# Scores of each batch's last 64 queries: four 64x64 products in place of two block-diagonal ones, in an attention + two-FFN kernel

## The chip, the cores and the metric

The kernel runs on one core of one Trainium2 chip. The metric is device time in microseconds (us) of one execution, the median of several runs; lower is better. The engines are named as in the profile: PE is TensorE's matmul, PEld its weight load, DVE is VectorE, ACT is ScalarE, POOL is GpSimd, SP issues DMAs.

## The reference

Four batches, eight heads, 576 positions, head size 64; then two feed-forward layers on the 2304 x 512 result.

```
scores = scale * q @ k.T                       # (4, 8, 576, 576), scale = 1/8
cum    = cumsum(max(s, 0))
scores = where(causal, -1e9, scores + min(-(cum_q - cum_k), 0))
attn   = softmax(scores) @ v
x = reshape(attn, (2304, 512))
x = ((x @ w_a) * (x @ w_b)) @ w_out            # d_ff 1536
h = x @ w_in                                   # d_ff 2048
out = (max(h, 0) + alpha * min(h, 0)) @ w_out2
```

## The kernel before

Positions are cut into four token blocks (512, 512, 512, 768 tokens). The feed-forward work of one block (`ffn`, and `ffn_seven` for the last block) is the stream that keeps PE busy; attention for the next block is fed into it in small steps. `attention(blk)` lists the steps for block blk: with a = blk, the first 512 queries of batch a (row blocks 0 to 3 of 128 queries: `s01`, `s23`), and with b = blk - 1, the last 64 queries of batch b (`s4`). Once the probabilities are ready, `two_av` or `av_b` multiplies them by v. The last batch's `s4` steps ride in the third block's stream, so the fourth block has no attention in it.

The change is about `s4(b, hp)`: the last QB = 64 queries of a batch, for a pair hp of heads, against all S = 576 keys. There are 4 batches x 4 pairs = 16 such steps. The pair's two heads lie on partitions 0 to 63 and 64 to 127 of the tile `kq` (columns 0 to 575 the keys, columns 576 to 703 the queries). The host lays the queries out block-diagonally (`last` in `kernel()`): columns 576 to 639 hold head 0's queries on partitions 0 to 63 and zero below, columns 640 to 703 hold head 1's on partitions 64 to 127 and zero above. So one 128x128 stationary operand gives both heads' scores, head j on output rows 64j to 64j+63. The keys go through in two halves of 288 columns, each into a PSUM bank of its own (L741). Operands are plain float32.

`soften` takes the scores out of PSUM. Its inner function `first()` issues one `tensor_tensor_reduce` per bank (L697): z = z - 0.125 * scores, with the row minimum into a column of `mn`; the issue is through the helper `dve`, so it shows up as L292 in the trace, as a CUSTOM_DVE_ANT_0 on z and a DVE_READ_ACCUMULATOR2_ANT on mn. With two columns in `mn`, one more 128x1 minimum joins them (L705). `rest()` does the exponential on ACT, the sum's reciprocal and the scaling; `turned` transposes on DVE (`zt`) and sends the result through DRAM (`zd`).

The order in which instructions are issued is made by a planner, `Order`, at build time. Each piece of work is a chain with a cost per engine (for a DVE operation of n elements, `run.dve + rate * n` ns with run.dve 90 or 155), and `run.pe(ns)` moves the planner's PE clock forward and lets it issue whatever fits (`pump`). From the second block on, a step is issued only when its inputs and its banks look ready by that clock (`possible`); feed-forward work goes ahead otherwise. `slot()` hands out PSUM banks from a ring: eight of them in the first attention, two (banks 0 and 1) afterwards; a bank is free again when its `reader` chain has ended.

Other PE lines that the prediction uses: L1248 to L1250 are the three products (high and low parts) of one feed-forward tile, 512 columns each, on the whole array. L557 and L563 (`q_k`) are the first batches' scores with 64 rows per head, so the two heads take one half of the array's rows each, into one bank each. L862 and L801 are probabilities times v with 128 rows and 64 output columns, the two heads on one half of the array's columns each.

Of the kernel before, what the change touches and what calls it, by code (L numbers as in the profile page):

```python
# [16 lines left out]
ALU = mybir.AluOpType  # L17
# [4 lines left out]
P = 128  # L22
# [4 lines left out]
BIG = 3.0e38  # L27
# [184 lines left out]
def attention_two_moe_kernel(  # L212
# [10 lines left out]
    nc = tc.nc  # L223
    B, S, _ = v.shape
# [8 lines left out]
    QB = S - QA  # L233
# [31 lines left out]
    run = Order()  # L265
# [8 lines left out]
    def act(o, i, func=AF.Copy, **k):  # L274
        yield {"act": run.act + 0.833 * size(o) + 93 * len(set(k) - {"scale"})}, SEEN
        nc.scalar.activation(o, i, func, **k)  # L276
# [13 lines left out]
    def dve(n, rate, f, *args, port=False, **k):  # L290
        yield {"dve2" if port else "dve": run.dve + rate * n}, SEEN
        f(*args, **k)  # L292
# [15 lines left out]
    def scale(o, i, s0, s1):  # L308
        n = size(o)
        eng = yield either(115 + 1.09 * n, dve2=run.dve + 0.52 * n), SEEN  # L310
        (nc.gpsimd if eng == "pool" else nc.vector).tensor_scalar(  # L311
            o, i, s0, s1, op0=ALU.mult, op1=ALU.mult
        )
# [123 lines left out]
    def slot():  # L437

        ring.append(ring.pop(0))
        if ring[-1] in reader:  # L440
            run.need(reader[ring[-1]])
        return ring[-1]
# [194 lines left out]
    def turned(b, h, rs, z):  # L637

        yield of_zt
        n = z.shape[1] // P  # L640
        zt = work.tile([P, 4 * n * 32], F32, name="zt", tag="zt", bufs=ZT)
        zd = dram.tile([4, P, n * 32], F32, name="zd", tag=f"zd{n}", bufs=8)
        yield from dve(
            n * P, 1.04, nc.vector.transpose, zt.rearrange("p (j t n) -> p j t n", j=4, n=32),
            z.rearrange("p (t j n) -> p j t n", j=4, n=32),
        )
        run.give(of_z[rs[0]], run.t)
        yield from dma(
            zd.rearrange("i (k j) m -> (i k) (j m)", j=4), zt
        )  # L650
        run.give(of_zt, run.t)
        if rs[0] == 4:
            yield of_pb
            pb_t[h] = raw.tile([P, 5 * P], F32, name="pb", tag="pb")
            o = pb_t[h].rearrange("p (i m) -> p i m", i=4)
        else:
            s0 = rs[0] * (rs[0] + 1) // 2 * 32
            o = pts[h % 4].rearrange("p (i m) -> p i m", i=4)[:, :, s0:s0 + n * 32]
        yield from dma(o, zd.rearrange("i p m -> p i m"))

    def soften(b, h, rs, srcs, *banks_read):

        got, masked = z_t[b, h, rs[0]]
        run.need(masked)
        z = got[0]
        k = len(rs)
        mn = small.tile([P, 2], F32, name="mn", tag="mn")
        sm = small.tile([P, 2], F32, name="sm", tag="sm")
        parts = []
        c = 0  # L670
        for i in rs:
            n = min(S, P * (i + 1))
            parts.append(z[:, c:c + n])
            c += n

        def rest():
            for i, p in enumerate(parts):
                yield from act(
                    p, p, AF.Exp, bias=mn[:, i:i + 1], scale=-1.0, accum_out=sm[:, i:i + 1]
                )  # L680
            for i in range(k):
                yield from dve(
                    1, 1, nc.vector.tensor_scalar, sm[:, i:i + 1], sm[:, i:i + 1], 1e-9, None,
                    op0=ALU.add,
                )
            yield from dve(1, 1, nc.vector.reciprocal, sm[:, 0:k], sm[:, 0:k])
            for i, p in enumerate(parts):
                yield from scale(p, p, sm[:, i:i + 1], 1.0)
            if b + (rs[0] == 4) >= TURN:
                e_t[b, h, rs[0]] = run.spawn(turned(b, h, rs, z), run.t)  # L690

        def first():
            c = 0
            for i, src in enumerate(srcs):
                n = src.shape[-1]
                p = z[:, c:c + n]
                yield from dve(  # L697
                    n, 1.04, nc.vector.tensor_tensor_reduce, p, src,
                    mask[:, QA - n:] if b < SUMS_PE and rs[0] < 4 else p, -0.125, BIG, ALU.add,
                    ALU.min, mn[:, i:i + 1],  # L700
                )
                c += n
            if len(parts) < len(srcs):
                yield from dve(
                    1, 1, nc.vector.tensor_tensor, mn[:, 0:1], mn[:, 0:1], mn[:, 1:2],  # L705
                    op=ALU.min, port=True,
                )
            if (b, h, rs[0]) == (SUMS_PE - 1, H - 1, 3):
                for i in range(KL):
                    run.give(of_kl, run.t)  # L710
            z_t[b, h, rs[0]] = z, run.spawn(rest(), run.t)

        got = run.spawn(first())
        z_t[b, h, rs[0]] = z, got
        for i in banks_read:
            reader[i] = got
# [16 lines left out]
    def s4(b, hp):  # L733


        got, ready = kq_t.pop((b, hp, 1))
        run.need(ready)
        at = [slot(), slot()]
        dst = [banks[i][:, 0:S // 2] for i in at]
        for j, d in enumerate(dst):  # L740
            nc.tensor.matmul(  # L741
                d, got[0][:, S:S + P], got[0][:, j * S // 2:(j + 1) * S // 2], start=True, stop=True
            )
            run.pe(4 * S // 2 / 2.4)
        run.give(of_kq)
        soften(b, hp, (4,), dst, *at)

# [184 lines left out]
    def attention(blk):  # L932
# [25 lines left out]
        for i in range(HP + 1):  # L958
# [9 lines left out]

            if has_a and a >= TURN:
                add(s4, i, b, i)  # L970
                add(s01, i, a, i)
                add(loads, i + 1, i + 1)
# [12 lines left out]
            elif has_a:  # L985
                add(s01, i, a, i)
                add(both, i, a, i, (2,))
                turns(0)
                add(both, i, a, i, (3,))
                add(s23, i, a, i, 2)  # L990
                last(j, 0)
                turns(1)
                last(j, 1)
                add(s23, i, a, i, 3)
                add(biases, i, b, i, (4,))
                add(loads, i + 1, i + 1)
                turns(2)
                add(both, i + 1, a, i + 1, (0, 1))
                add(two_av, j, a, b, j, blk)
                add(s4, i, b, i)  # L1000
            else:
                add(loads, i + 1, i + 1)
                add(s4, i, b, i)
                add(biases, i + 1, b, i + 1, (4,))
                last(i, 0)
                last(i, 1)
                if i == HP:
                    steps.extend([(lambda: None, ())] * TAIL)
                add(av_b, i - (blk >= TURN), b, i - (blk >= TURN), blk)
# [899 lines left out]
    for blk in range(NB):  # L1909
# [11 lines left out]
        if 1 <= blk < NB - 1:  # L1921
            n = max(0, blk * S + QA - blocks[blk + 1][0])
# [72 lines left out]
```

## Time and profile before

| | us |
|---|---|
| median of 3 runs | 984.69 (983.88 to 987.27) |
| span of the profiled execution (first to last instruction) | 982.3 |
| PE busy | 963.1 (98%) |
| DVE busy | 748.5 (76%) |
| ACT busy | 558.7 (57%) |
| POOL busy | 223.7 (23%) |

The profile gives the span of the profiled execution as its own time and shows nothing around it; the median of the runs is 2.4 us longer than that span. PE's matmuls overlap in the records (the end of each is modelled), so the start of one to the start of the next is the time that it costs, not its length. A timeline line with x4 is four records in a row of the same source line, and its first number is the start of the first.

### The profile page before, as it was taken

The numbers are of one execution on the slowest core, as the hardware profiler recorded it, in microseconds if no ns is written. First come the engines' busy times: TensorE is split into PE (matmuls) and PEld (weight loads), VectorE is DVE, ScalarE is ACT, GpSimd is POOL, SyncE is SP. The second block draws the span as 40 slices with busy tenths as digits, with TensorE's granted clock in tenths as the row PEclk, the third lists the DMA queues.
The fourth block names the chain that finished last, engine by engine and source line by source line (L and its number), as shares of the span: only waits on it lengthen the run. The fifth ranks groups of instructions, "written<-read, shape, count | busy, mean of one in ns | idle before, by whom it ended". The sixth has DMA issues, their size and how long they took to land.

```text
span 982.3 us, 15862 instructions
## 1 busy us (share of the span) xinstructions
PE 963.1 (98%) x5235; PEld 810.3 (82%) x5235; DVE 748.5 (76%) x1743; ACT 558.7 (57%) x1173; POOL 223.7 (23%) x290
## 2 busy tenths in 40 slices
PE   6989999999999999999999999999999999999998
PEld 5557787778888878888888888888899999999997
DVE  7777886986878788888478868666497888787782
ACT  6856675775855555665455547544552333476453
POOL 2131110431124234563135434522100000000000
PEclk9999999999999999999999999999999999999999
DMA  7589999899788979688388785855402212112101
GB/s 181 185 262 320 347 332 322 293 323 329 245 271 259 304 245 312 194 257 293 112 270 260 218 264 194 251 172 183 165 22 94 78 66 87 43 47 82 61 5 65
DMA packets 140083, 196.78 MB, mean 200 GB/s; under 512 B 35744, under 2 KB 79776, under 8 KB 140000
## 3 DMA queue, kind: packets, MB, share of 16 engines
q1 hardware_dynamic: 130208, 177.93, 58.0%
q10 hardware_dynamic: 9792, 17.83, 4.9%
q8 instruction: 41, 0.67, 0.3%
q14 instruction: 42, 0.34, 0.1%
HBM read 152.13 MB, written 43.59 MB: 199 GB/s over the span
## 4 chain that ended last, share of the span: by engine, by line
PE 84%; DMA 8%; DVE 5%; issue 1%; ACT 1%; SPq 0%; POOL 0%; ACTq 0%; DVEq 0%
PE bank L1248 18%; PE bank L1249 18%; PE bank L1250 18%; PE bank L1886 5%; PE bank L1888 4%; PE bank L1887 4%; DMA cb<-cum_d 3%; PE bank L1735 2%; PE bank L1734 2%; PE bank L1736 2%; PE bank L801 2%; DMA raw<-in_w_dram 2%; PE bank L563 2%; PE bank L544 1%; PE bank L741 1%
## 5 line engine op out<-in xcount | busy, mean ns | idle before, releaser
L1248 PE MATMUL bank<-xh,wh 128*128 128x512 f32 (+1 forms) x620 | 237.9, 384 | 2.0 <-DVE g L292 2.0
L1250 PE MATMUL bank<-xh,wl 128*128 128x512 f32 (+1 forms) x620 | 234.0, 377 | 0.0
L1249 PE MATMUL bank<-xl,wh 128*128 128x512 f32 (+1 forms) x620 | 234.0, 377 | 0.0
L284 ACT ACTIVATE wh<-raw 128x512 fp32r<-128x512 f32 (+1 forms) x198 | 115.1, 592 | 84.4 <-PE bank L1249 35.0
L1248 PEld LDWEIGHTS bank<-xh,wh 128*128 128x128 f32 x620 | 116.4, 188 | 26.1 <-issue 4.6
L1250 PEld LDWEIGHTS bank<-xh,wl 128*128 128x128 f32 x620 | 116.4, 188 | 19.3
L1249 PEld LDWEIGHTS bank<-xl,wh 128*128 128x128 f32 x620 | 116.4, 188 | 18.6
L301 POOL TENSOR_TENSOR wl<-raw,wh 128x512 fp32r<-128x512 f32 x69 | 91.5, 1329 | 110.9 <-ACT wh L284 71.1
L301 DVE TENSOR_TENSOR wl<-raw,wh 128x512 fp32r<-128x512 f32 (+1 forms) x135 | 84.6, 640 | 33.7 <-ACT wh L284 27.8
L276 ACT ACTIVATE z<-z,mn 128x512 f32<-128x512 f32 (+4 forms) x144 | 82.8, 577 | 47.3 <-DVE mn L292 45.9
L1248 PE MATMUL bank<-gh,wh 128*128 128x512 f32 (+1 forms) x240 | 89.5, 373 | 0.0
L1249 PE MATMUL bank<-gl,wh 128*128 128x512 f32 (+1 forms) x240 | 88.7, 370 | 0.4 <-DVE gl L301 0.2
L1250 PE MATMUL bank<-gh,wl 128*128 128x512 f32 (+1 forms) x240 | 88.5, 369 | 0.0
L284 ACT ACTIVATE gh<-g 128x512 fp32r<-128x512 f32 x84 | 52.8, 629 | 43.5 <-DVE g L292 40.1
L1886 PE MATMUL bank<-wh,gh 128*128 128x512 f32 x192 | 76.4, 398 | 0.0
L1029 ACT ACTIVATE top<-raw 128x512 f16<-128x512 bf16 x90 | 68.5, 784 | 12.3 <-DMA raw<-in_w_dram 10.9
L1888 PE MATMUL bank<-wh,gl 128*128 128x512 f32 x192 | 74.8, 389 | 0.0
L1887 PE MATMUL bank<-wl,gh 128*128 128x512 f32 x192 | 74.8, 389 | 0.0
L301 DVE TENSOR_TENSOR gl<-g,gh 128x512 fp32r<-128x512 f32 x69 | 51.6, 748 | 18.8 <-ACT gh L284 18.0
L292 DVE STREAM_TRANSPOSE zt<-z 128x384 f32<-128x384 f32 (+2 forms) x88 | 55.7, 648 | 2.4 <-DMA zd<-zt 1.4
L616 POOL TENSOR_SCALAR_AFFINE_SELECT z<-z 64x64 f32<-64x64 f32 (+2 forms) x80 | 34.0, 432 | 97.3 <-DVE z L606 63.7
L311 DVE TENSOR_SCALAR z<-z,sm 128x512 f32<-128x512 f32 (+4 forms) x100 | 55.0, 573 | 1.3
(151 smaller groups left out, 1918.1 us busy)
## 6 DMA issues: line engine op xcount, KB each, us to landing
raw<-w_d SPq DMA_DIRECT2D x91, 512.0 KB, 4.3
raw<-in_w_dram SPq DMA_DIRECT2D x90, 512.0 KB, 5.6
w_d<-w ACTq DMA_DIRECT2D x46, 256.0 KB, 5.0
zd<-zt SPq DMA_DIRECT2D x48, 192.0 KB, 5.0
pt<-zd SPq DMA_DIRECT2D x48, 192.0 KB, 4.9
kq<-in_kq_a_dram SPq DMA_DIRECT2D x16, 512.0 KB, 5.7
vb<-in_v_dram SPq DMA_DIRECT2D x112, 64.0 KB, 4.4
zd<-zt SPq DMA_DIRECT2D x24, 256.0 KB, 4.0
```

The costliest lines, as they stand in the source:

```text
L276: nc.scalar.activation(o, i, func, **k)
L284: nc.scalar.activation(o, i, AF.Copy, scale=by)
L292: f(*args, **k)
L301: (nc.gpsimd if eng == "pool" else nc.vector).tensor_tensor(o, i0, i1, op=ALU.subtract)
L311: (nc.gpsimd if eng == "pool" else nc.vector).tensor_scalar(o, i, s0, s1, op0=ALU.mult, op1=ALU.mult)
L1029: nc.scalar.activation(top.bitcast(F16).rearrange("p (n t) -> p n t", t=2)[:, :, 1], r.bitcast(BF16)[:, 4:4 + 4 * WN].rearrange("p (n t) - ...
L1248: nc.tensor.matmul(o, wh, ih, start=first, stop=False)
L1249: nc.tensor.matmul(o, wh, il, start=False, stop=False)
L1250: nc.tensor.matmul(o, wl, ih, start=False, stop=last)
L1886: nc.tensor.matmul(acc[t], gh[:, c], wh, start=first, stop=False)
L1887: nc.tensor.matmul(acc[t], gh[:, c], wl, start=False, stop=False)
L1888: nc.tensor.matmul(acc[t], gl[:, c], wh, start=False, stop=last)
```

## The change

In `s4`, two products on the whole array (128 rows, 128 columns, 288 keys each) become four on quarters of it: head j's 64 rows of kq, its 64 query columns (the non-zero block), and one half k of its keys, written to bank j on partitions 64k to 64k+63. The planner is told of one `run.pe` of 480 ns where it was told of two. In `first()`, the scores now lie by head in the banks and by key half on the partitions, so z is read head by head and half by half: four `tensor_tensor_reduce` of 64 partitions x 288 in place of two of 128 x 288, each writing the same z and the same two columns of mn as before on its 64 partitions. No DMA, tile or buffer changes.

```diff
         def first():
+            if rs[0] == 4:
+                halves = [slice(i * QB, (i + 1) * QB) for i in range(2)]
+                n = S // 2
+                for own, src in zip(halves, srcs):
+                    for i, part in enumerate(halves):
+                        p = z[own, i * n:(i + 1) * n]
+                        yield from dve(
+                            n, 1.04, nc.vector.tensor_tensor_reduce, p, src[part], p, -0.125, BIG,
+                            ALU.add, ALU.min, mn[own, i:i + 1],
+                        )
             c = 0
-            for i, src in enumerate(srcs):
+            for i, src in enumerate(srcs if rs[0] < 4 else ()):
                 n = src.shape[-1]
...
         dst = [banks[i][:, 0:S // 2] for i in at]
-        for j, d in enumerate(dst):
-            nc.tensor.matmul(
-                d, got[0][:, S:S + P], got[0][:, j * S // 2:(j + 1) * S // 2], start=True, stop=True
-            )
-            run.pe(4 * S // 2 / 2.4)
+        for k in range(2):
+            for j, d in enumerate(dst):
+                own = slice(j * QB, (j + 1) * QB)
+                nc.tensor.matmul(
+                    d[k * QB:(k + 1) * QB], got[0][own, S + j * QB:S + (j + 1) * QB],
+                    got[0][own, k * S // 2:(k + 1) * S // 2], start=True, stop=True,
+                )
+        run.pe(4 * S // 2 / 2.4)
         run.give(of_kq)
         soften(b, hp, (4,), dst, *at)
```

## Rows read from the trace of the kernel before

**Rows 1.** The page: busy time by engine, and the chain that ended last.

```profile
PE 963.1 (98%) x5235; PEld 810.3 (82%) x5235; DVE 748.5 (76%) x1743; ACT 558.7 (57%) x1173; POOL 223.7 (23%) x290
...
PE 84%; DMA 8%; DVE 5%; issue 1%; ACT 1%; SPq 0%; POOL 0%; ACTq 0%; DVEq 0%
```

**Rows 2.** Busy time by stretch of 50 us; PE, PEld, DVE, ACT, POOL, clock, DMA.

```profile
250.00:300.00 50.00, 50.00 (x272) 41.64 (x271) 38.97 (x85) 33.43 (x66) 10.38 (x13) 1.00 0.83 283
300.00:350.00 50.00, 50.00 (x272) 41.61 (x271) 39.25 (x96) 25.86 (x56) 18.06 (x26) 1.00 0.88 264
```

**Rows 3.** What PE waited for: us in total, times, longest.

```profile
PE bank L1248 <- DVE g L292: 2.0, 1, 2.0
...
PE bank L544 <- DVE ovl L301: 0.8, 1, 0.8
...
PE bank L1249 <- DVE gl L301: 0.2, 1, 0.2
```

**Rows 4.** The products of L741: count, ns (min/median/max), first and last start.

```profile
L741 PE MATMUL bank<-kq x64: 404/406/408, 48.1 to 678.7; 128*128 128x288 f32 x64
```

**Rows 5.** PE's timeline around one s4 step before: start, length, line.

```profile
314.79 0.39 PE L1250 MATMUL bank<-xh,wl 128*128 128x512 f32 x1
315.02 1.13 PE L741 MATMUL bank<-kq 128*128 128x288 f32 x4
315.77 0.61 PE L1248 MATMUL bank<-gh,wh 128*128 128x512 f32 x1
316.22 0.39 PE L1249 MATMUL bank<-gl,wh 128*128 128x512 f32 x1
```

**Rows 6.** PE's timeline around products on the row halves, 384 and 512 keys.

```profile
149.04 0.39 PE L1250 MATMUL bank<-xh,wl 128*128 128x512 f32 x1
149.36 0.44 PE L557 MATMUL bank<-cums,rows 64*128 64x384 f32 x2
149.64 0.81 PE L563 MATMUL bank<-kq 64*128 64x384 f32 x4
...
150.72 0.40 PE L1249 MATMUL bank<-gl,wh 128*128 128x512 f32 x1
...
167.67 1.02 PE L563 MATMUL bank<-kq 64*128 64x512 f32 x4
...
168.96 0.39 PE L1249 MATMUL bank<-xl,wh 128*128 128x512 f32 x1
```

**Rows 7.** PE's timeline of products on the column halves.

```profile
344.98 0.80 PE L862 MATMUL bank<-pb,vb 128*64 128x64 f32 x20
345.61 2.35 PE L801 MATMUL bank<-pt,vb 128*64 128x128 f32 x40
```

**Rows 8.** DVE's timeline from the first s4's scores to the late g.

```profile
54.58 0.45 DVE L292 CUSTOM_DVE_ANT_0 z<-bank,z 128x288 f32<-128x288 f32 x1
...
54.95 0.45 DVE L292 CUSTOM_DVE_ANT_0 z<-bank,z 128x288 f32<-128x288 f32 x1
...
55.33 0.28 DVE L292 CUSTOM_DVE_ANT_0 z<-bank,mask 128x128 f32<-128x128 f32 x1
...
66.25 0.58 DVE L292 STREAM_TRANSPOSE zt<-z 128x384 f32<-128x384 f32 x1 [1.39 <-DMA zd<-zt]
...
69.88 0.67 DVE L292 TENSOR_TENSOR g<-bank,a_sb 128x512 f32<-128x512 f32 x1
```

**Rows 9.** DVE by form: the s4 read; then two subtractions, min/median/max ns.

```profile
L292 DVE CUSTOM_DVE_ANT_0 z<-bank,z 128x288 f32<-128x288 f32 x32 | 13.6, 446 | 0.6 <-PE bank L741 0.5
...
L301 DVE TENSOR_TENSOR gl<-g,gh x69: 646/692/1786, 72.1 to 704.1; 128x512 fp32r<-128x512 f32 x69
...
L301 DVE TENSOR_TENSOR qs<-kq,qs x10: 689/690/1674, 263.7 to 595.6; 64x512 fp32r<-64x512 f32 x10
```

**Rows 10.** PE's timeline, first block: a wait for a load, and for g.

```profile
52.36 0.37 PE L563 MATMUL bank<-kq 64*128 64x128 f32 x1 [2.60 <-DMA kq<-in_kq_a_dram]
...
70.61 0.50 PE L1248 MATMUL bank<-xh,wh 128*128 128x512 f32 x1 [2.04 <-DVE g L292]
```

## Prediction, made before the changed kernel was run

> **What bounds the kernel now.** I read the page first. PE is busy 98% of the span and 84% of the chain that ended last is PE [rows 1]: PE is the engine to shorten, if that busy time is real and not a wait in disguise. The view by stretches of 50 us, read next, shows PE at 50.00 of 50 in the middle of the kernel at a granted clock of 1.00 (2.4 GHz), while DVE works 39 us of each 50 [rows 2]. The list of PE's waits then says how little is lost there: after the first 60 us it has three entries, 2.0, 0.8 and 0.2 us, 3.0 us together, all for DVE [rows 3]. So between 70 and 700 us a nanosecond off PE is a nanosecond off the end, and a DVE operation costs nothing until something that PE needs is behind it. The last read is PE's timeline, line by line, around the step that changes and around steps that already use half the array; the price comes from there, start to start.
>
> **Removed: the two whole-array products.** There are 64 records for 16 steps, four each [rows 4]: a float32 product shows as two records. In the step at 315 us the first record starts at 315.02 and the second feed-forward product after it at 316.22 [rows 5], 1.20 us later; without the step that distance would be one feed-forward product, 315.02 - 314.79 = 0.23. The step costs 0.97 us of PE.
>
> **Added: four quarter products.** No row shows quarters of the array, so I build the price from halves. With 64 rows per product and the two heads side by side, 384 keys take from 149.64 to the second product after them at 150.72, 1.08 - 0.23 = 0.85 us; 512 keys take 168.96 - 167.67 - 0.23 = 1.06 us [rows 6]. The difference, 0.21 us for 128 keys more, is 1.64 ns a key. The whole-array step pays 0.97 us for two products of 288 keys, 1.68 ns a key for each. So two half-array products together pay for one: they run side by side. The column halves do it too: twenty records of 64 columns take 345.61 - 344.98 = 0.63 us [rows 7], 0.49 ns a column and record, against 0.97/(4 x 288) = 0.84 when records follow one another [rows 5]. There the two halves stream different data through the same 128 rows, as the two key halves will through the same 64.
>
> If all four quarters run at once, 288 keys cost 0.85 - 96 x 1.64 ns = 0.69 us by the row halves. In that are 288 x 1.64 = 0.47 us of streaming and 0.22 us of leaving the split array: the first full product after it is slow to start. Entering it costs too: 149.36 - 149.04 = 0.32 in place of 0.23, so 0.09 us [rows 6]. For the two extra tiles I add 0.02 us; the bounds are 0 and, at the 0.03 us a record of the column halves [rows 7] for four loads in a row, 0.13. Sum 0.69 + 0.09 + 0.02 = 0.80 us, bounds 0.78 to 0.91. A step gains 0.17 us (0.06 to 0.19), not the half that four-for-two suggests: changing the shape of the array twice eats 0.31 us of 0.48.
>
> The Trainium skill, "TensorE: Matmul & The Clock Gate", Part 3 (Measured speedup vs the span model), gives a pack of tiles the duration of one product plus about 4 ns for each further tile, with nothing for entering or leaving. By it the step would cost about 0.5 us. The trace of the halves disagrees: it shows 0.31 us more for the two changes of shape.
>
> The first of the 16 steps, at 48.1 us [rows 4], gains nothing: PE waits for a load of keys right after it, until 52.36 [rows 10]. For the other 15 the next line is a full-array product and PE has no wait to hide the gain in. Gain on PE: 15 x 0.17 = **2.6 us** (0.9 to 2.9).
>
> **Added: two DVE reads per step.** Two CUSTOM_DVE reads of 128x288 become four of 64x288. The mean length is 0.446 us [rows 9], but back to back they start 0.37 and 0.38 us apart, accumulator read included [rows 8]. Half the partitions don't make one shorter: a subtraction of 64x512 has a median of 690 ns and one of 128x512 692 [rows 9]. So each step adds 2 x 0.375 = 0.75 us of DVE (0.75 to 1.06: with the full length and a separate accumulator read of 0.08), 12 us over 16 steps. Reading from other partitions than it writes has no row; I put it at nothing, inside those bounds. What hides it: DVE idles 11 us of each 50 [rows 2], and 16 steps in 630 us add 1.0 us to each 50. If the cover is gone, each 0.75 that stands ahead of a `g` or `gl` which PE waits for lands on PE in full.
>
> One place has no cover. The first step's scores are read from 54.58, DVE then works almost without pause, and the `g` at 69.88, in the same queue, ends when PE has been waiting for it: 2.04 us at 70.61 [rows 8, 10]. The only gap on the way, 1.39 us before 66.25, waits for a transfer of `zt` [rows 8], and the first of those transfers comes from this same step, so it moves along. I take the full **+0.75 us** here; it would be 0 if that transfer keeps its time, 1.06 at most. Behind the added reads in DVE's queue stand also the remaining softmax of the step (exp on ACT waits for the minimum), the weight splits and the transposition; their users come several feed-forward tiles later. The two banks stay occupied 0.75 us longer; the next step that wants them is usually further off than that. For small delays elsewhere, at the two other waits [rows 3], I add **0.3 us** (0 to 1.5).
>
> **Moved.** No DMA is added or moved between queues. The keys' buffer comes free 0.17 us sooner. The planner's clock advances 480 ns less per step while PE really gains 170, and its DVE cost grows by 0.8 to 0.9 us: from the first step on it may place steps and choices of engine differently. That can remove a wait of [rows 3] or add one; I price it at nothing, with 1.5 us either way.
>
> **Sum.** -2.6 + 0.75 + 0.3 = -1.55 us. The profiled execution's span, 982.3, becomes 980.75; it stands 2.4 under the median, and I carry the difference over: 984.69 - 1.55 = **983.1 us**. A measurement of this kernel can tell about 0.3% from no change, 2.95 us, so below 981.74 is faster and above 987.64 slower. The forecast is no change, with a small gain underneath.
>
> **The rivals.**
>
> *DVE becomes the bound of PE (slower).* Where: at the starts of blocks and around each step, when `gl` is read soon after it is written. Price 0.75 us each time it lands; the gain is used up after 4 of 16, and it is slower by over 0.3% from (2.6 + 2.95)/0.75 = 7.4, so 8 of 16. With 10 of 16: 984.69 - 2.6 + 7.5 = 989.6. For it: all of PE's late waits are for DVE [rows 3]. Against: 3.0 us in all, and 22% of DVE idle. 15%. The Trainium skill, "TensorEngine Tiling (Array Packing)", PSUM Bottleneck, warns that tiling speeds up TensorE but not the emptying of PSUM. Here the emptying even takes twice the instructions; [rows 2] show the room for it.
>
> *The quarters don't run four at a time, but two (slower).* The change would then not do what it says: 2 x 0.47 + 0.22 + 0.09 + 0.02 = 1.27 us a step, 0.30 more than now, 15 x 0.30 + 0.75 + 0.3 = +5.6, so 990.2. Against: both kinds of halves run in pairs [rows 6, 7], and four quarters together read and write no more per column than two column halves do. 7%.
>
> *The new order loses the waits (faster).* The gain at its bound, 2.9, and half or more of the 3.0 us of waits gone, the one at 70 included: 984.69 - 2.9 - 1.5 = 980.3. For it: it takes one `g` issued two operations earlier. Against: DVE has more ahead of it there. 24%.
>
> *The whole 0.48 us is gained (faster).* 16 x 0.48 - 0.75 = 6.9, so 977.8. Against: the 0.31 us of entering and leaving are in the rows of the halves [rows 6]. 4%. This is the case that the Trainium skill's span model, quoted above, would give.
>
> **How the numbers follow.** The forecast has 50%; its own range is 981.8 to 986.0 (from 2.9 gained and nothing lost, to 0.9 gained and 2.2 lost). All of it lies within 0.3%. Faster: 24 + 4 = 28%. Slower: 15 + 7 = 22%. Same: 50%. The range 980.0 to 989.0 holds the forecast, most of the lost waits and the smaller half of the DVE rival; it leaves out two-at-a-time, the whole gain and the worst of the DVE rival.
>
> **What would show it.** Right: eight records of 64*64 per step with the four first ones starting within about 0.03 us; from the first to the second feed-forward product behind, 0.69 + 0.02 + 0.23 = 0.94 us (1.20 before); 64 CUSTOM_DVE of 64x288 near 0.446 us; the wait at 70 us grown to about 2.8; the sum of PE's late waits under 5 us. Wrong: quarter records whose starts lie 0.24 us apart and more in pairs (two at a time), a new PE wait for DVE of over 1 us after a step (DVE rival), or no slow product after the step (whole gain).

## The result and the profile after

The changed kernel takes 991.74 us (median of 5; 988.92 to 992.89) against 984.75 us (median of 5): ratio 1.0059, 95% interval 1.0039 to 1.008. It is slower by 7.0 us. The forecast was no change at 983.1; the measured time is outside the stated range too.

First the page of the changed kernel, busy time and chain. PE's work has hardly grown, but its share of the chain is down from 84% to 79% [rows 1], and ACT, DVE and "issue" have come in: PE now waits.

```profile
PE 965.4 (97%) x5299; PEld 803.2 (81%) x5299; DVE 746.7 (75%) x1780; ACT 562.3 (57%) x1182; POOL 247.2 (25%) x308
...
PE 79%; DMA 8%; DVE 6%; ACT 3%; issue 3%; SPq 0%; POOL 0%; ACTq 0%; DVEq 0%; POOLq 0%
```

Then the step itself, in PE's timeline (L753 are the quarter products; L1261 to L1263 are the feed-forward lines L1248 to L1250 of before), and the products by count, ns (min/median/max) and first and last start.

```profile
323.06 0.39 PE L1263 MATMUL bank<-xh,wl 128*128 128x512 f32 x1
323.37 0.72 PE L753 MATMUL bank<-kq 64*64 64x288 f32 x8
324.02 0.50 PE L1261 MATMUL bank<-gh,wh 128*128 128x512 f32 x1
324.35 0.39 PE L1262 MATMUL bank<-gl,wh 128*128 128x512 f32 x1
```

```profile
L753 PE MATMUL bank<-kq x128: 402/428/454, 48.6 to 687.8; 64*64 64x288 f32 x128
```

The four quarters run at once. From the start to the second product after it is 0.98 us (1.20 before [rows 5]); with the entry, 323.37 - 323.06 - 0.23 = 0.08, the step costs 0.98 - 0.23 + 0.08 = 0.83 to 0.84 us against 0.97. That gain of 0.13 us stands after 15 of the 16 steps, 1.9 us together, in every one of them alike. So the loss isn't in the products.

PE's waits (us in total, times, longest) show where it is. These are the changed kernel's, 9.3 us with two short ones, of 0.4 and 0.3 us, that aren't shown; one of the three for `mn` in the first line, 0.85 us at 58.28, lies ahead of 60 us, so 8.4 us come after it, where before had 3.0 [rows 3].

```profile
PE bank L557 <- DVE mn L292: 3.5, 3, 1.9
...
PE bank L557 <- DVE ovl L301: 2.6, 1, 2.6
...
PE bank L1899 <- ACT gh L284: 1.5, 1, 1.5
...
PE bank L875 <- DVE mn L292: 0.8, 1, 0.8
...
PE bank L1261 <- DVE g L292: 0.2, 1, 0.2
```

PE's timeline around the largest, in the first block (the first line is the wait ahead of 60 us):

```profile
58.28 0.97 PE L557 MATMUL bank<-cums,rows 64*128 64x512 f32 x2 [0.85 <-DVE mn L292]
...
80.83 0.32 PE L557 MATMUL bank<-cums,rows 64*128 64x128 f32 x1 [1.93 <-DVE mn L292]
81.82 0.47 PE L557 MATMUL bank<-cums,rows 64*128 64x128 f32 x1 [0.67 <-DVE mn L292]
...
83.82 0.79 PE L1261 MATMUL bank<-xh,wh 128*128 128x512 f32 x1
...
85.27 0.63 PE L1261 MATMUL bank<-gh,wh 128*128 128x512 f32 x1
...
87.83 0.52 PE L1261 MATMUL bank<-gh,wh 128*128 128x512 f32 x1
...
172.94 2.07 PE L563 MATMUL bank<-kq 64*128 64x512 f32 x4
174.95 0.79 PE L1261 MATMUL bank<-xh,wh 128*128 128x512 f32 x1
...
177.30 0.39 PE L1261 MATMUL bank<-xh,wh 128*128 128x512 f32 x1
```

Behind the wait come nine feed-forward products in 87.83 - 83.82 = 4.01 us, 0.43 us each from 85.27 on, where 0.23 is normal: the granted clock is 0.50 there, the lower level, 1.2 GHz. Nine products and 0.11 us for leaving the split array would be 2.15 us at the upper one, so the fall costs 1.9 us on these nine. It began ahead of them: from the second L557 at 81.82 to the first of the nine it takes 2.00 us, where the whole of the same step before took 83.13 - 82.05 = 1.08 us, so at least 0.9 us more.

```profile
82.05 0.33 PE L557 MATMUL bank<-cums,rows 64*128 64x128 f32 x2
...
83.13 0.50 PE L1248 MATMUL bank<-xh,wh 128*128 128x512 f32 x1
```

The same happens after the wait for `ovl` that ends at 172.94: L563 takes 2.01 us where it took 0.95 (from 167.67 [rows 6] to 168.62), and the next six products 2.35 in place of 1.47, 1.9 us again. Added up from 60 us on: -1.9 (the steps), +5.4 (waits, 8.4 - 3.0), +4.7 (clock) = +8.2. When each feed-forward product's start is compared with the same one's before, the changed kernel is 0.7 us ahead at 60 us and 8.1 behind at 700, a loss of 8.8 us, so 0.6 of it is not accounted for.

**Who was late.** DVE's timeline at the first wait, and ACT's at the second:

```profile
72.30 0.68 DVE L292 TENSOR_TENSOR g<-bank,a_sb 128x512 f32<-128x512 f32 x1
79.22 0.71 DVE L292 STREAM_TRANSPOSE zt<-z 128x512 f32<-128x512 f32 x1 [6.23 <-DMA zd<-zt]
79.85 0.41 DVE L292 CUSTOM_DVE_ANT_0 z<-bank,z 64x288 f32<-64x288 f32 x1
...
80.31 0.46 DVE L292 CUSTOM_DVE_ANT_0 z<-bank,z 64x288 f32<-64x288 f32 x1
...
80.81 0.45 DVE L292 CUSTOM_DVE_ANT_0 z<-bank,z 64x288 f32<-64x288 f32 x1
...
81.30 0.46 DVE L292 CUSTOM_DVE_ANT_0 z<-bank,z 64x288 f32<-64x288 f32 x1
```

```profile
171.78 0.77 ACT L1042 ACTIVATE top<-raw 128x512 f16<-128x512 bf16 x1 [3.27 <-DMA raw<-in_w_dram]
...
172.43 0.20 ACT L284 ACTIVATE ovh<-bank 128x64 fp32r<-128x64 f32 x1
```

In neither is the engine overloaded. DVE stands idle for 6.23 us behind a transposition that waits for a transfer to free its buffer, with the new reads, for whose banks PE waits, queued behind it. ACT stands idle behind a weight tile that hasn't landed, with the copy that would free PE's bank queued behind that. Both are in the main a matter of what stands where in the queues. A part of the first is the new work: PE's second wait there, 0.67 us until 81.82, is for the last of the four reads, which start 0.46 to 0.50 us apart where the two before started 0.37 and 0.38 apart [rows 8]. SP's queue shows the loads; from 57 us on, the changed kernel first, then before:

```profile
57.66 0.53 SPq L317 DMA_DIRECT2D raw<-in_w_dram  x1
...
61.46 6.89 SPq L317 DMA_DIRECT2D zd<-zt  x3
...
71.09 1.60 SPq L317 DMA_DIRECT2D raw<-in_w_dram  x2
```

```profile
60.77 0.33 SPq L317 DMA_DIRECT2D raw<-in_w_dram  x1
...
63.71 0.57 SPq L317 DMA_DIRECT2D raw<-in_w_dram  x1
64.43 2.75 SPq L317 DMA_DIRECT2D zd<-zt  x3
...
70.87 1.41 SPq L317 DMA_DIRECT2D raw<-in_w_dram  x2
```

After the one at 57.66, which before issues at 60.77, the changed kernel issues no weight load until 71.09; before issues one more at 63.71. The lag is one load at 65 us (10 against 11, counted from the start) and grows to four at 120 and at 150 (23 against 27, 33 against 37). The stretches of 30 us (columns as in [rows 2]; the last two are the DMA engines' busy share and GB/s) show what that means, the changed kernel first, then before:

```profile
60.00:90.00 30.00, 27.40 (x117) 21.19 (x117) 21.19 (x61) 15.73 (x35) 10.21 (x15) 0.89 0.86 274
90.00:120.00 30.00, 30.00 (x180) 23.44 (x179) 22.38 (x47) 17.47 (x33) 4.68 (x6) 1.00 0.92 274
120.00:150.00 30.00, 30.00 (x145) 23.82 (x144) 24.48 (x63) 21.16 (x41) 6.96 (x7) 1.00 0.99 331
```

```profile
60.00:90.00 30.00, 27.96 (x128) 21.72 (x126) 27.02 (x76) 19.65 (x42) 8.87 (x12) 1.00 0.94 311
90.00:120.00 30.00, 30.00 (x180) 23.42 (x180) 23.17 (x51) 18.71 (x36) 2.77 (x4) 1.00 1.05 327
120.00:150.00 30.00, 30.00 (x142) 24.04 (x140) 23.27 (x55) 20.98 (x40) 5.19 (x6) 1.00 0.99 337
```

In the first block the DMA engines are busy throughout in the kernel before (0.94 to 1.05). The changed kernel is behind by 30 us x (37 + 53 + 6) GB/s = 2.9 MB at 150 us and hasn't made it up by 175 (299 against 325 GB/s from 60 us on). Its own engines have room until 120 us (0.86 and 0.92; 0.73 at 234 GB/s from 60 to 78 us, ahead of the first long wait), so it is the transfers that start late. How much of PE's waits comes from that, the experiments ask; a part of the lag is itself an effect of PE being 2.7 us late from 89 us on.

### The profile page after: what moved, and what is told of

It reads as the page before. It is cut to its first block, busy times and chain, and to the rows that moved or that the text cites. A ratio compares the mean times of both kernels' runs of the same rounds, so it can differ in the third digit from the quotient of the medians.

```text
span 990.4 us, 16076 instructions
## 1 busy us (share of the span) xinstructions
PE 965.4 (97%) x5299; PEld 803.2 (81%) x5299; DVE 746.7 (75%) x1780; ACT 562.3 (57%) x1182; POOL 247.2 (25%) x308
## 4 chain that ended last, share of the span: by engine, by line
PE 79%; DMA 8%; DVE 6%; ACT 3%; issue 3%; SPq 0%; POOL 0%; ACTq 0%; DVEq 0%; POOLq 0%
PE bank L1261 18%; PE bank L1262 18%; PE bank L1263 18%; PE bank L1899 4%; DMA raw<-in_w_dram 4%; PE bank L1901 4%; PE bank L1900 4%; PE bank L1748 2%; PE bank L1747 2%; PE bank L1749 2%; PE bank L814 2%; PE bank L544 2%; DVE z L292 2%; DMA cb<-cum_d 2%; DMA w_d<-w 1%
## 5 line engine op out<-in xcount | busy, mean ns | idle before, releaser
L1261 PE MATMUL bank<-xh,wh 128*128 128x512 f32 (+1 forms) x620 | 238.0, 384 | 0.2 <-DVE g L292 0.2
L1263 PE MATMUL bank<-xh,wl 128*128 128x512 f32 (+1 forms) x620 | 234.5, 378 | 0.0
L1261 PEld LDWEIGHTS bank<-xh,wh 128*128 128x128 f32 x620 | 116.7, 188 | 28.7 <-issue 7.7
L1263 PEld LDWEIGHTS bank<-xh,wl 128*128 128x128 f32 x620 | 116.7, 188 | 19.5
L301 POOL TENSOR_TENSOR wl<-raw,wh 128x512 fp32r<-128x512 f32 x78 | 103.7, 1332 | 110.1 <-ACT wh L284 81.6
L301 DVE TENSOR_TENSOR wl<-raw,wh 128x512 fp32r<-128x512 f32 (+1 forms) x126 | 79.2, 644 | 27.3 <-ACT wh L284 26.2
L1261 PE MATMUL bank<-gh,wh 128*128 128x512 f32 (+1 forms) x240 | 89.7, 374 | 0.0
L1263 PE MATMUL bank<-gh,wl 128*128 128x512 f32 (+1 forms) x240 | 88.9, 371 | 0.0
L292 DVE CUSTOM_DVE_ANT_0 z<-bank,z 64x288 f32<-64x288 f32 (+3 forms) x128 | 57.7, 469 | 12.7 <-PE bank L544 8.0
L284 ACT ACTIVATE wh<-w 128x512 fp32r<-128x512 f32 x67 | 41.3, 627 | 26.5 <-DVE w L292 11.1
```

The source lines that it names most:

```text
L284: nc.scalar.activation(o, i, AF.Copy, scale=by)
L301: (nc.gpsimd if eng == "pool" else nc.vector).tensor_tensor(o, i0, i1, op=ALU.subtract)
L1261: nc.tensor.matmul(o, wh, ih, start=first, stop=False)
L1263: nc.tensor.matmul(o, wl, ih, start=False, stop=last)
```

## The experiments

**Theory A**: the changed kernel loses by its new issue order. The planner was told of 480 ns less PE time and of two more DVE operations per step, and from the first step on it placed everything else differently. **Theory B**: the added work loses it, the two more reads per step and the banks that they hold. Later, within A: **A1**, the order costs in the first block, through the full DMA engines; **A2**, any new order costs, wherever it is.

### The new work in the old order

```diff
+                    yield {"dve": run.dve + 1.04 * n}, SEEN        # one told cost for two reads
+                    for i, part in enumerate(halves):
+                        nc.vector.tensor_tensor_reduce(p, src[part], p, ...)
...
         for k in range(2):
...
+            run.pe(4 * S // 2 / 2.4)                               # told twice, as before
```

> The four quarter products and four reads of the change, but the planner is told the old costs (two run.pe of 480 ns, two DVE links, each of which issues two reads), so that every engine's queue stands in the order of the kernel before, with two reads in the place of one. Theory A (the changed kernel loses by its new issue order): PE gains 15 x 0.13 = 1.9 us, the read delay costs up to 0.75 us once and little elsewhere, so 983.0 to 984.5, against 984.8 before. Theory B (the extra reads themselves and the banks they hold cost PE its time): the waits of the changed kernel come back, 989 to 992.

Measured: 984.54 us, ratio 1.0003 (0.9989 to 1.0017). All queues stand as in the kernel before, with two reads in each read's place. The 7 us are gone and the new work is all there: theory B falls as the cause of the 7 us. But the gain on PE isn't to be seen in the time either. To place it I compare the start of the same feed-forward product in two traces (this comparison is meant below wherever a loss has a place). Against before, this run is 0.7 us ahead at 156 us, 1.1 us behind at 174, 1.2 behind at 191 and level at 684: the steps gain, and one stretch of the first block took it away. (That stretch varies from one execution to the next: in the last experiment below, whose program is the kernel before's up to 190 us, 0.8 us are lost there too.) Of its waits from 59 us on, all small, these matter most:

```profile
PE bank L544 <- DVE ovl L301: 1.2, 1, 1.2
...
PE bank L557 <- DVE mn L292: 1.0, 1, 1.0
...
PE bank L1261 <- ACT gh L284: 0.6, 1, 0.6
...
PE bank L1261 <- DVE g L292: 0.5, 1, 0.5
```

### The old work in the new order

```diff
+                    yield from dve(n, 1.04, nc.vector.tensor_tensor_reduce, p, src, p, ...)
+                    yield {"dve": run.dve + 1.04 * n}, SEEN        # told, nothing issued
...
             nc.tensor.matmul(d, got[0][:, S:S + P], ...)
-            run.pe(4 * S // 2 / 2.4)
+        run.pe(4 * S // 2 / 2.4)
```

> The two whole-array products and two reads of the kernel before, but the planner is told the costs of the change (one run.pe of 480 ns, four DVE links, two of which issue nothing), so that every engine's queue stands in the order of the changed kernel. Theory A (order): the waits of the changed kernel stay, about 8 to 10 us of them with the clock that falls after them, and the PE gain of 1.9 us is not there: 991 to 994. Theory B (work): no extra reads, no loss: 984 to 986.

Measured: 989.38 us, ratio 1.0042 (1.0027 to 1.0057). With none of the new work, the new order alone costs 4.6 us. That is theory A's direction, below its number. The changed kernel has 2.4 us more, which the two intervals just allow; but by theory A alone it would have 1.9 us less than this run, for its gain on PE, and that they hardly allow. So in the new order the new work isn't shown to be free: the four reads' part in the wait at 81.82 is one place where it costs.

### One told number

```diff
         for j, d in enumerate(dst):
             nc.tensor.matmul(...)
-            run.pe(4 * S // 2 / 2.4)
+        run.pe(4 * S // 2 / 2.4)
```

> The kernel before with one line moved: the planner's PE clock is told of 480 ns per step in place of 960; products, reads and their told cost are the old ones. Theory A in a general form (any new order from this planner costs some us): 986 to 992, with PE waits of over 1 us that before does not have. Theory A in a narrow form (only a larger told DVE cost leads to a bad order): 984 to 986. Theory B: 984 to 986, since no work is added.

Measured: 991.29 us, ratio 1.0061 (1.0038 to 1.0084). Products, reads and their costs are those of before; only the planner's PE clock is told 480 ns less per step, and a loss of 6.5 us is back. PE's longest waits after 60 us, two of them:

```profile
PE bank L557 <- DVE ovl L301: 4.5, 2, 3.2
```

### The four reads, done and told, with the old products

```diff
+                for own in halves:
+                    for i, src in enumerate(srcs):
+                        p = z[own, i * n:(i + 1) * n]
+                        yield from dve(n, 1.04, nc.vector.tensor_tensor_reduce, p, src[own], p, ...)
```

> The whole-array products of the kernel before, with two run.pe as before, and the four reads of 64x288, done and told. Theory A: a third order, with waits of its own, 985 to 992. Theory B: the reads are what costs, so 990 to 993 (the changed kernel without its PE gain).

Measured: 991.37 us, ratio 1.0063 (1.0043 to 1.0083). Both theories allowed that. It has to be read with the next one.

### The four reads in the old order

```diff
+                for own in halves:
+                    yield {"dve": run.dve + 1.04 * n}, SEEN
+                    for i, src in enumerate(srcs):
+                        p = z[own, i * n:(i + 1) * n]
+                        nc.vector.tensor_tensor_reduce(p, src[own], p, ...)
```

> The old whole-array products, the four reads of 64x288, and the old order and old told costs: the reads alone. Theory A: the new work in the old order came to no change with a PE gain of 15 x 0.127 = 1.9 us in it, so the reads alone cost about 1.9 us: 986 to 987.5. If the reads cost PE nothing and the quarter products don't gain either: 984 to 985.

Measured: 984.24 us, ratio 1.0007 (0.9988 to 1.0026). The same 64 reads that went with +6.6 us when told cost nothing measurable when the queues don't move. I had expected them to eat the 1.9 us of PE; the two intervals, each 1.4 to 1.9 us either way, are too wide to say whether they eat a part. These reads write the partitions that they read, and so come a little closer together than the changed kernel's (the point on the reads, below); the first experiment has those.

### Old costs, or new costs, for the first batch's steps alone

The changed kernel's work in both; `told old` stands for the costs as in the first experiment, for b == 0 in one kernel and for b > 0 in the other.

```diff
+                        if i == 0 or not (b == 0):                 # the mirror image: not (b > 0)
+                            yield {"dve": run.dve + 1.04 * n}, SEEN
...
+            if k or (b == 0):
+                run.pe(4 * S // 2 / 2.4)
```

> The changed kernel's work everywhere; the planner is told the old costs for the first batch's four steps (they run in the first block, up to 190 us) and the new ones for the twelve others, so that the queues stand as before up to there and in a new order after. Theory A1 (the new order costs in the first block, where the DMA engines are full and late weight loads can't be made up): as with the old order throughout, plus at most 1 us, 984 to 986, and no clock fall. Theory A2 (any new order costs, wherever it is): the waits after 190 us, 2 to 4 us, stay, 986 to 989.

> The mirror image: new costs told for the first batch's four steps, old ones for the others; the changed kernel's work everywhere. PE's own order is that of the kernel before. Theory A1: most of the changed kernel's loss, 988 to 991, with DMA busy under 0.9 in 60 to 90 us. Theory A2: about half the loss, 986 to 988. If PE's order were what counts: 983 to 985.

Measured: 986.26 us, ratio 1.0027 (1.001 to 1.0045), with the old order up to 190 us; 990.84 us, ratio 1.008 (1.0048 to 1.0112), with the new costs told for the first batch alone. PE's own order in the second is that of before. So the first block's order makes the larger part of the loss, and the order of PE's instructions isn't what does it; but with the old order up to there, the new one after 190 us still shows losses of 1.7 us at 268 to 283 us and 1.0 us at 600 to 618, so A1 alone is too narrow. DMA busy in the first block, second kernel (the execution of 995.83 us; 0.86 in the next 30 us):

```profile
60.00:90.00 30.00, 26.09 (x113) 20.09 (x112) 20.29 (x58) 14.95 (x33) 9.26 (x13) 0.89 0.80 261
```

### A truer cost for the old kernel

```diff
-            run.pe(4 * S // 2 / 2.4)
+            run.pe(486.5)
```

> The kernel before, with the second of a step's two PE costs told as 486.5 ns, which is what a product takes, in place of 480; nothing else. PE's order stays the same, the other queues' order moves. Theory A with costs that are told wrongly as the cause: 984 to 985.5, since these are truer. Theory A with any other order as the cause: 986 to 992.

Measured: 987.34 us, ratio 1.0043 (1.0024 to 1.0061). A told cost that is 6.5 ns off the old one and nearer to the truth, and PE's order unchanged: 2.9 us slower by the medians (the ratio makes it 4.2). Its one large wait is at 67 us, in the first block:

```profile
67.25 0.71 PE L1248 MATMUL bank<-xh,wh 128*128 128x512 f32 x1 [3.50 <-ACT a_sb L284]
```

So the planner needs no false numbers to lose: a new order of the other queues is enough. Late loads are not what cost this run: its weight loads are issued no later than before's (18 against 16 by 90 us, 27 against 27 by 120). No kernel here whose queues were reordered came out as fast as the one before.

### More bytes in the old order

```diff
-            nc.scalar.dma_start(w_d[i].bitcast(I32), source[0])
+            if 8 <= n < 23:                                        # nine stores write their 256 KB twice
+                two_w = source[0].rearrange("p (o n) -> p o n", o=1).to_broadcast([P, 2, WN])
+                nc.scalar.dma_start(w_d[i].bitcast(I32).rearrange("o p n -> p o n"), two_w)
```

> The kernel before, every queue in its old order, but nine of the first block's weight write-backs (the 9th to 23rd weight tiles) write their 256 KB twice, by the same instruction: 2.36 MB more, a little less than the 2.8 MB that the changed kernel is behind by 150 us. The second copy is never read; nothing else of the computation changes. Theory A1 (the first block is bound by the DMA engines, and bytes that are late by 150 us come out as PE waits at 155 to 175 us): 988 to 992, with PE waiting for ovl or gh in that stretch and ACT waiting there for raw. If the DMA engines have slack: 984 to 986.

Measured: 988.85 us, ratio 1.0043 (1.0026 to 1.0061). The size is as A1 has it, 4.4 us for 2.4 MB. The place isn't: the loss falls at 117 us, not at 155 to 175, in the same kind of step, L557 waiting for `ovl`:

```profile
117.09 0.49 PE L557 MATMUL bank<-cums,rows 64*128 64x512 f32 x1 [2.19 <-DVE ovl L301]
```

So bytes in the first block cost time. But a busy share of 1.0 was not the most that the engines move: here they move 346 and 361 GB/s in the two stretches from 90 to 150 us (shares 1.07 and 1.03), where before moves 327 and 337.

### The weight loads earlier in the changed kernel

```diff
-SL_LOAD, SL_PARTS, SL_QK, SL_BIAS = 10000.0, 5000.0, 5000.0, 2500.0
+SL_LOAD, SL_PARTS, SL_QK, SL_BIAS = 2500.0, 5000.0, 5000.0, 2500.0
```

> The changed kernel with one planner constant, the slack given to weight loads (SL_LOAD), at 2500 in place of 10000, which puts the first block's weight loads at least as early in SP's queue as before (the 11th to 20th at places 42 to 80 of it; before 48 to 83, changed kernel 55 to 85). Theory A1: the DMA engines are fuller from 60 to 120 us and the waits at 155 to 175 us shrink by 2 us or more: 984 to 988.5. Theory A2 (any order but the old one costs 6 us): 990 to 993.

Measured: 987.75 us, ratio 1.0033 (1.002 to 1.0046): 3.3 us are left of the 7.0, by one constant and with the changed work. In its trace (the execution of 989.81 us) the loss at 77 to 100 us is 1.4 us in place of 5.8 and that at 156 to 176 us is 1.1 us in place of 4.0, but one of 5.9 us at 110 to 125 us is new, again L557 behind `ovl`, so the time is A1's and the path is not. The DMA engines are fuller only from 60 to 90:

```profile
60.00:90.00 30.00, 28.77 (x136) 21.63 (x135) 23.90 (x69) 17.93 (x36) 14.99 (x17) 1.00 0.93 293
90.00:120.00 30.00, 27.32 (x161) 20.36 (x159) 20.86 (x47) 17.14 (x37) 6.10 (x9) 0.94 0.91 278
```

### The new work where the DMA engines aren't full

```diff
+            new = rs[0] == 4 and b > 0
...
+        if b > 0:                                                  # quarters; else the two old products
```

> Old order and old costs told; the first batch's four steps as in the kernel before, the quarter products and four reads only for the other twelve. If the gain on PE is real and its loss in the run with the old order sat in the first block: 12 x 0.127 = 1.5 us less than before and at most 0.5 us of new waits, 982.8 to 984.0 against 984.8. If the reads cost as much later on too: 984.5 to 986.

Measured: 985.81 us, ratio 1.0015 (0.9996 to 1.0033). This didn't show what it was for. The profiled execution's span, 981.6, is 0.7 below before's 982.3, the median of the runs is above; a gain of 1.5 us doesn't stand out from runs that spread over several. The trace does show the gain arriving behind the first block: product by product it goes from level with before at 191 us to 0.7 us ahead at 684, though one loss of 1.0 us at 319 to 340 (L544 waits 0.9 for `mn`) lies between. Whether the quarter products ever shorten the kernel stays open. No version measured faster than the kernel before.

## Why the prediction was wrong, point by point

- **The step's price.** Right in kind: four at a time, with the price of entering and leaving taken from the halves. 0.84 us against 0.80, inside its bounds, so 1.9 us of gain in place of 2.6. Half the records are 0.05 us longer than the others (454 and 402 ns): I had added 0.02 us for the two extra tiles, and that was probably the undersized term. The span model of the Trainium skill's page "TensorE: Matmul & The Clock Gate" (Part 3), about 0.5 us, doesn't hold here as the price of the step: start to start it is 0.84 us, with the way in and the way out.
- **The DVE reads.** The length was right: 64 reads with a mean of 453 ns (first line below), half the partitions no shorter. The price was too low: they follow one another 0.46 to 0.50 us apart (79.85 to 81.30 above), not 0.375, so four, with their accumulator reads, hold DVE from 79.85 to 81.77, 1.92 us, where the two of the same step before hold it from 78.77 to 79.61, 0.84: 1.1 us more, just above the bounds of 0.75 to 1.06. "Reading from other partitions than it writes ... at nothing" was the undersized term. In the run with the reads alone, where a read writes the partitions that it reads, the second of a pair starts 0.38 us after the first, and only the next, on the other partitions, 0.46 (the other lines).

```profile
L292 DVE CUSTOM_DVE_ANT_0 z<-bank,z 64x288 f32<-64x288 f32 x64 | 29.0, 453 | 4.6 <-PE bank L753 3.1
```

```profile
77.69 0.44 DVE L700 CUSTOM_DVE_ANT_0 z<-bank,z 64x288 f32<-64x288 f32 x1
...
78.07 0.45 DVE L700 CUSTOM_DVE_ANT_0 z<-bank,z 64x288 f32<-64x288 f32 x1
...
78.53 0.46 DVE L700 CUSTOM_DVE_ANT_0 z<-bank,z 64x288 f32<-64x288 f32 x1
```

- **The place with "no cover".** One trace can't judge it: I put 0.75 us on the wait for `g` at 70 us, and with the reads in the old order that wait is 0.5 us, not 2.8. But it varies from one execution to the next by more than that: in the last experiment, with before's program up to there, it is 0.88 us, not 2.04.

```profile
69.78 0.50 PE L1269 MATMUL bank<-xh,wh 128*128 128x512 f32 x1 [0.88 <-DVE g L292]
```

- **"Moved: I price it at nothing, with 1.5 us either way".** This is the step that failed. I had seen that the planner would be told 480 ns less per step and 0.8 us more of DVE, and that it could place things differently, and treated that as noise around zero. The runs put it at +4.6 us with no new work at all, at +6.5 us for the PE number alone, and at +2.9 us for a change of 6.5 ns. All of them are losses.
- **Why it only lost.** That the order costs the time is shown; by which path is argued. The sum had PE as the one full resource. In [rows 2], at 250 to 350 us, it is; the prediction took no row from the stretches from 60 to 175 us, where the DMA engines are as busy as PE. My reading is that a load that stands a few places later in SP's queue isn't caught up there, and that the waits come out tens of us later on ACT and DVE, with PE behind. For it: the first block's order alone brings back 6.4 us, and 2.4 MB more cost 4.4. Against it as the whole story: the truer cost lost 2.9 us with loads that were not late, and the extra bytes cost their time at another place than the late loads did. The range's 1.5 us had no row from that stretch under it.
- **The rivals.** "DVE becomes the bound of PE" named the right waiters (all its waits after 60 us are for DVE or ACT), and its sign came true, a new wait for DVE of over 1 us after a step; but most of its reason is wrong: DVE idles for 6.23 us ahead of that one, and the added reads are in it with the 0.67 us at 81.82. "Two at a time" and "the whole gain" are out by the timeline. "The new order loses the waits" had the sign reversed: it put new ones in, 1.9, 2.6, 1.5 and 0.8 us, and PE's late waits come to 8.4 us where under 5 was the sign of being right. The 2.04 us of `g` are 0.2 here, as that rival has it, but an unchanged program has shown 0.88 as well. The Trainium skill's page "TensorEngine Tiling (Array Packing)", PSUM Bottleneck, points at the emptying of PSUM; the runs with the reads in the old order (984.54 and 984.24 us) show it to be no bottleneck there.
- **What stays open.** How much of the loss is the late loads and how much the transpositions standing ahead of reads in DVE's queue: more bytes alone give 4.4 us, earlier loads give back 3.7 of 7.0, and with the old order in the first block 1.8 us of loss remain, where DMA isn't short (0.83 at 250 to 300 us [rows 2]). Whether another order in the changed kernel would turn the 1.9 us on PE into time was not found.

## What to carry to other kernels

In a kernel whose instruction order is planned from told costs, a change has two parts, the work and the order that its costs bring about; run them apart (new work under old costs, old work under new costs) before judging the work. Before pricing a reorder at nothing, look at every stretch, not the middle alone, for a second resource that is busy throughout: here the DMA engines, at 0.94 to 1.05 in the first block, where the new order cost most. Compare executions of an unchanged program before reading a wait of 1 or 2 us out of one trace. And a split of the array pays by what is left after entering and leaving it, here 0.13 us of a hoped-for 0.48.

## What the runs showed of the hardware that I had not expected

- **A wait can cost PE twice.** After the waits at 78 to 82 us and 170 to 173 us the granted clock fell to its lower level, and at least 2.8 and some 1.9 us were lost behind the waits themselves (0.89 in the stretch 60 to 90 us above), nearly as much as the waits. The 2.0 us wait before [rows 10] had been followed by no fall: its stretch from 60 to 90 us shows 1.00. The length of a wait alone doesn't tell whether the clock falls: in the run with more bytes one of 2.62 us for `g` at 70.8 us was followed by none (1.00 from 60 to 90 us), and the one of 2.19 at 117.09 by a fall (0.50 from 117.6 to 121).
- **Reads on DVE that change partitions start later.** 0.46 to 0.50 us apart in the changed kernel, where each reads other partitions than the one before it, against 0.38 when a read of the same size stays on the same ones (77.69 to 78.07 above). The reason was not looked for.
- **Four quarters started together aren't quite one product.** Their records come in two lengths, 454 and 402 ns, where those of the whole array in [rows 4] have one, 404 to 408; the step is 0.04 us longer than the halves had led me to expect. Why was not tried.
